# Weight differences formed in the attention part, and a third expert computed by quarter products

## The chip, the core and the metric

The kernel runs on one core of a Trainium2 chip. The core has a matrix engine (TensorE, PE in the profile), a vector engine (VectorE, DVE), a scalar engine (ScalarE, ACT), GpSimd (POOL) and a sync engine (SP); each has its own queue of instructions, and SP's queue here does nothing but issue DMAs. The metric is the device time of one launch in microseconds, as the median of several runs. A profile of one further execution shows each instruction with its times.

## The reference

```python
x = attention(q_l, k_l, v_l, q_g, k_g, v_g)     # 8 x 544 tokens, 512 columns
P = sinkhorn(exp(x @ w_gate), 8 rounds)          # 4352 tokens x 8 experts
out = 0
for e in range(8):
    h = maximum(x @ w1[e], 0)                    # 512 -> 1024
    out += P[:, e:e+1] * (h @ w2[e])             # 1024 -> 512
```

The attention has 8 batches of 8 heads with 512 local and 32 global positions; the local queries see a band of 32 positions on each side and the global ones. The routing matrix `P` multiplies every expert's output, so all eight experts work on all tokens.

## The kernel before

**First part.** A loop over 32 steps `s` (8 batches of 4 head pairs, `HP = 4`) does the attention. It is written out by hand: each step issues scores, exponentials, transposes and value products for three neighbouring head pairs on the engines, and at fixed places `f1(...)` puts in a piece of the first layer of experts 0 to 3, whose hidden rows `hT` (line 471 on ACT, 473 on DVE) are kept for later: `hd<-hT` on SP, line 475. The loads of the next batch are issued at the end of a step. The first layers' weights of experts 4 to 7 are copied into a 16-bit array in DRAM, `w1d`, by `load_w1d`, one expert in each of the batches 3 to 6. `hT` tiles, and some others, take turns in the four slots of `hpool` (tag `hT`). Then come the sinkhorn rounds, with the rest of the first layers of experts 0 to 3 between them.

**Second part.** 72 units (m, e): nine groups `m` of 512 tokens (the last has 256), and in each the experts in `ORDER = (4, 0, 5, 1, 6, 2, 7, 3)`. Even units are the experts 4 to 7, whose first layer is still to be computed; odd units are the experts 0 to 3, whose hidden rows are loaded from DRAM (`load_h`) and scaled by `P` (`scale_h`, one DVE instruction of 4.4 us, or two halves). An even unit and the odd one after it are called a pair here. While the second layer of a pair runs on PE (`product`, line 928, seven products `q` for each unit after a Strassen-like scheme), the first layer of the next even unit is put between its products. Ahead of a unit's products DVE forms its sums (`sums`: two instructions into `s`, part 0, and two in place in `h`, part 1). The results stand in seven PSUM banks over a whole group; with the last odd unit of a group (`closes`) ten DVE instructions (`add`, line 944) bring them into the output tile. The first product of the next group into a bank waits for the bank's `add`.

The first layer of an even unit can be done in two ways:

- *plain* (`l1`, line 818): 32 matmuls of 512 columns, each block evacuated by ACT;
- *by quarter products* (`Fast`, line 836): two halves `p`, each of 7 products of 4 matmuls of 256 columns. The half `p = 0` runs within the even unit of the pair before, `p = 1` within the odd one. It needs four differences of its inputs on DVE (`sums_x`: tiles `t5`, `t6`, `t4` and one in place) and seven blocks of weights and weight differences, loaded as one tile `w1q` from `w1c`. In each half `s0` forms the products H and Q, ACT copies both (`K`, line 852; `t5`, line 854), `s1` goes on in K and in H, and DVE then writes X = H + `t5` (line 861). `s2` goes on in the same bank H, which X reads, and DVE writes Y (line 868); `s3` ends H.

`fast(i)` tells which units take the second way: by `WX = {6: 2, 7: 2}` those of experts 6 and 7 from group 2 on, 12 units. The four blocks of weight differences of each of the experts 6 and 7 and each half are made in group 1: four loads of 128 KB into a slot of `w1e` (line 726), four DVE instructions (`prep_w1`, by the helper `tt`, line 689), and a store to `w1c` on GpSimd's queue (line 741).

The order of the work is that of the program text. The tile framework only adds the waits. If a unit is plain and the next even one is by quarter products, the even step's order is:

```python
if not fast(i):
    sums(i + 1, part=(0,))      # DVE
f.s0(); product(i, 3); f.s1()   # X on DVE at the end of s1
product(i, 4); product(i, 5)
f.s2()                          # PE, in the bank that X reads
```

Of the kernel before, what the change touches and what calls it, by code (L numbers as in the profile page):

```python
# [9 lines left out]
FP16 = mybir.dt.float16  # L10
FP32 = mybir.dt.float32
AF = mybir.ActivationFunctionType
ALU = mybir.AluOpType
# [10 lines left out]
def kernel(  # L24
# [13 lines left out]
    nc = tc.nc  # L38
# [3 lines left out]
    D, E = moe_w_gate.shape  # L42
    F = moe_w1.shape[2]
    P = 128
# [6 lines left out]
    HP = H // 2  # L51
# [23 lines left out]
    xd = [ydram.tile([P, DP, n], FP16, name=f"xd{m}") for m, (_, n) in enumerate(groups)]  # L75
    w1d = [ydram.tile([P, DP, F], FP16, name=f"w1d{e}") for e in range(NL, E)]
    pd = ydram.tile([E, NTOK], FP32, name="pd")
    WX = {6: 2, 7: 2}
    w1c = {e: [ydram.tile([P, 7, 2, 256], FP16, name=f"w1c{e}_{p}") for p in range(2)] for e in WX}
    psx = ExitStack()  # L80
    xpool = psx.enter_context(tc.tile_pool(name="xpool", bufs=1, side="right"))
# [10 lines left out]
    with tc.tile_pool(name="att_c", bufs=1) as att_c, \  # L92
# [308 lines left out]
        def st_G1(b, g):  # L401
            n0 = HP * b + 2 * g
            qg = qgbd[(2 * b + g) % 2]
            gc = slice(Sg * b, Sg * (b + 1))
            sg = ps_po.tile([P, 2 * 512], FP32, tag="po")
            for c0, c1, k0 in ((0, Sl - W, 2 * W), (Sl - W, Sl, W), (Sl, S, None)):
                for pr in range(2):
                    rhs = kgT[:, 2 * g + pr, gc] if k0 is None else kTe[(n0 + pr) % NK][:, k0 : k0 + c1 - c0]
                    nc.tensor.matmul(sg[:, c0:c1], qg[:, pr, :], rhs, start=(pr == 0), stop=(pr == 1))
            m2 = att_wk.tile([P, 4], FP32, tag="m2")  # L410
            nc.vector.reduce_max(out=m2[:, 0:1], in_=sg[:, 0:S], axis=AX.X)  # L411
            nc.vector.tensor_scalar(out=m2[:, 1:2], in0=m2[:, 0:1], scalar1=-scale, scalar2=None, op0=ALU.mult)
            Pg = att_wk.tile([P, S], FP16, tag="Pg")
            nc.scalar.activation(out=Pg, in_=sg[:, 0:S], func=AF.Exp, scale=scale, bias=m2[:, 1:2],
                                 accum_out=m2[:, 2:3])
            gs[(b, g)] = (Pg, m2)
# [60 lines left out]
        def load_w1e(e):  # L477
# [2 lines left out]
            wts[e] = pool.tile([P, DP, F], FP16, name="w1e", **kw)  # L480
            nc.gpsimd.dma_start(out=wts[e], in_=moe_w1[e].rearrange("(dko dki) f -> dki dko f", dki=P))

        def load_w1d(e):
            nc.gpsimd.dma_start(out=w1d[e - NL], in_=moe_w1[e].rearrange("(dko dki) f -> dki dko f", dki=P))

        fill = [(k % NL, k // NL) for k in range(NL * (B + 1))]
        n1 = 0
# [100 lines left out]
        for s in range(HP, NU + 1):  # L588
# [65 lines left out]
                logits(NJ * ((s - 5) // HP), NJ)  # L654
            if g1:
                st_G1(*gn)
            if s < NU and b + 1 < B:
                if hp == 0:
                    load_qk(b + 1, 0, (nc.sync, nc.sync))
                    load_qk(b + 1, 1, (nc.sync, nc.sync))  # L660
                elif hp == 1:
                    cast_qk(b + 1, 0, gq)
                    if b >= NL - 1:
                        load_w1d(b + 1)
                elif hp == 2:
                    vq = load_v(b + 1)
                    run(vq[:3])
                    cast_qk(b + 1, 1, gq)
                else:
                    run(vq[3:])  # L670
# [17 lines left out]
    def tt(out, in0, in1, op):  # L688
        nc.vector.tensor_tensor(out=out, in0=in0, in1=in1, op=op)  # L689
# [16 lines left out]
        return i < NUN and units[i][0] < B and units[i][0] >= WX.get(units[i][1], B)  # L706

    wseq = [(i, p) for i in range(0, NUN, 2) for p in ((0, 1) if fast(i) else (None,))]
    for j, (e, p) in enumerate((e, p) for e in WX for p in range(2)):
        wseq.insert(wseq.index((E + 2 * j + 2, None)), (e, "raw", p))  # L710
    raw = {}
    wnext = 0

    def load_w1(used):
        nonlocal wnext
        while wnext < len(wseq) and (wnext < 2 or wseq[wnext - 2] in used):
            i, *p = wseq[wnext]
            if p[0] is None:
                w = w1s[i] = wpool.tile([P, DP, F], FP16, tag="w1e", name="w1s")
                nc.sync.dma_start(out=w, in_=w1d[units[i][1] - NL])  # L720
            else:
                w = wpool.tile([P, 7, 2, 256], FP16, tag="w1e", name="w1q")
                if p[0] == "raw":
                    for o, r, k in ((0, 0, 0), (1, 0, 1), (3, 1, 0), (2, 1, 1)):
                        f0 = 512 * r + 256 * p[1]
                        nc.sync.dma_start(out=w[:, o], in_=w1d[i - NL][:, 2 * k : 2 * k + 2, f0 : f0 + 256])
                    raw[wseq[wnext]] = w
                else:
                    nc.sync.dma_start(out=w, in_=w1c[units[i][1]][p[0]])
                    w1s[(i, p[0])] = w  # L730
            wnext += 1
            if wnext < 2:
                return

    def prep_w1():
        for k in list(raw):
            w = raw.pop(k)
            for o, a, b, op in ((5, 0, 3, ALU.subtract), (3, 3, 2, ALU.add), (4, 3, 0, ALU.subtract),
                                (6, 1, 4, ALU.subtract)):
                tt(w[:, o], w[:, a], w[:, b], op)  # L740
            nc.gpsimd.dma_start(out=w1c[k[0]][k[2]], in_=w)
            used.add(k)

    def load_pb(*us):
        us = [i for i in us if i < NUN]
# [327 lines left out]
    for i, (m, e) in enumerate(units):  # L1073
        if i == NUN - 1:
            last_pair(i)
        elif i % 2 == 0:
# [44 lines left out]
            else:  # L1121
# [1 line left out]
                h = hs[i + 1]  # L1123
                s = ss[i + 1] = xsp.tile([P, HF, n], FP16, tag="xs", name="sl")
                tt(s, h[:, 0:HF, 0:n], h[:, HF:FT, 0:n], ALU.add)
            if m > 0:
                prep_w1()
            scale_x(i + 4)
            if m == 0:
                for e in {2: (2,), 4: (7,), 6: (3,)}.get(i, ()):  # L1130
# [83 lines left out]
```

## Time and profile before

| what | value |
|---|---|
| median of 3 runs | 1045.3 us (1044.04 to 1048.0) |
| profiled execution, own time | 1044.08 us |
| its span in the trace | 1042.2 us |
| PE / DVE / ACT / POOL busy in the span | 97% / 83% / 49% / 13% |
| first part, to the last first-layer matmul of experts 0 to 3 | 0 to 396 us |
| groups 1 to 7 of the second part | 491 to 1017 us |

In the profile's listings, a row of a window gives its stretch, its length and the busy microseconds of PE, of PE's weight loads, of DVE, ACT and POOL with their numbers of instructions, then the granted share of PE's clock, the busy share of the DMA engines and what they moved in GB/s. A row of the chain gives start, length and work. A row of a timeline gives start, length, engine, line, operation, tiles, and in brackets the idle time ahead of it and what ended it. `L689` is the line of the helper `tt`, so DVE's `L689` rows are told apart by their tiles.

### The profile page before, as it was taken

The numbers are of one execution on the slowest core, as the hardware profiler recorded it, in microseconds if no ns is written. First come the engines' busy times: TensorE is split into PE (matmuls) and PEld (weight loads), VectorE is DVE, ScalarE is ACT, GpSimd is POOL, SyncE is SP. The second block draws the span as 40 slices with busy tenths as digits, with TensorE's granted clock in tenths as the row PEclk, the third lists the DMA queues.
The fourth block names the chain that finished last, engine by engine and source line by source line (L and its number), as shares of the span: only waits on it lengthen the run. The fifth ranks groups of instructions, "written<-read, shape, count | busy, mean of one in ns | idle before, by whom it ended". The sixth has DMA issues, their size and how long they took to land.

```text
span 1042.2 us, 22693 instructions
## 1 busy us (share of the span) xinstructions
PE 1015.2 (97%) x9142; PEld 728.5 (70%) x9142; DVE 868.7 (83%) x1638; ACT 513.0 (49%) x1296; POOL 139.7 (13%) x227
## 2 busy tenths in 40 slices
PE   7899999999999999999999999999999999999998
PEld 4555555555555466777777877877877878878887
DVE  7687777777776786999889799889899898898895
ACT  7777878787876675223222333333333332332331
POOL 7442423414312102000000000000000000000000
PEclk9899999999999999999999999999999999999999
DMA  9887588988945999946756546454553555464470
GB/s 260 197 217 207 118 273 181 220 232 177 258 136 142 275 261 302 259 143 203 272 194 234 189 153 219 160 189 180 200 189 138 203 187 168 172 218 152 145 260 26
DMA packets 101960, 206.08 MB, mean 198 GB/s; under 512 B 33936, under 2 KB 68192, under 8 KB 90592
## 3 DMA queue, kind: packets, MB, share of 16 engines
q1 hardware_dynamic: 56064, 162.75, 45.1%
q0 software_dynamic: 43184, 32.26, 17.7%
q10 hardware_dynamic: 2608, 9.64, 2.4%
q8 instruction: 71, 1.16, 0.4%
q14 instruction: 33, 0.27, 0.1%
HBM read 168.64 MB, written 57.29 MB: 217 GB/s over the span
## 4 chain that ended last, share of the span: by engine, by line
PE 83%; ACT 8%; DVE 6%; issue 2%; DMA 1%; SPq 0%; POOL 0%; ACTq 0%; DVEq 0%
PE m L928 28%; PE ph L818 15%; PE ph L468 15%; PE pm L928 11%; PE pf L836 7%; ACT Pu L311 4%; DVE Pu L348 3%; PE ptw L359 1%; ACT hT L471 1%; ACT qbd L285 1%; PE pv L157 1%; PE pt L275 1%; DMA vraw<-in_v_l_dram 1%; PE po L380 1%; DVE m L411 1%
## 5 line engine op out<-in xcount | busy, mean ns | idle before, releaser
L468 PE MATMUL ph<-xT,w1e 128*128 128x512 f16 (+1 forms) x1152 | 255.9, 367 | 0.2
L928 PEld LDWEIGHTS <-h 128*128 128x128 f16 x2160 | 211.4, 98 | 36.6
L820 ACT ACTIVATE h<-ph 128x512 f16<-128x512 f32 (+1 forms) x192 | 107.5, 562 | 204.2 <-PE ph L818 202.2
L928 PE MATMUL m<-w2c,s 128*128 128x256 f16 x1620 | 199.9, 273 | 0.0
L928 PEld LDWEIGHTS <-s 128*128 128x128 f16 x1620 | 158.5, 98 | 30.5
L818 PE MATMUL ph<-xs,w1s 128*128 128x512 f16 (+1 forms) x768 | 174.6, 361 | 0.0
L468 PEld LDWEIGHTS <-w1e 128*128 128x128 f16 x1152 | 105.4, 98 | 96.1 <-issue 3.0
L689 DVE TENSOR_TENSOR h<-h,pb 128x2048 f16<-128x2048 f16 (+1 forms) x48 | 152.4, 3175 | 3.8 <-DMA h<-hd 3.7
L689 DVE TENSOR_TENSOR s<-h 128x1024 f16<-128x1024 f16 (+2 forms) x166 | 126.4, 803 | 24.3 <-PE m L928 16.9
L928 PE MATMUL m<-w2c,h 128*128 128x256 f16 x1080 | 137.2, 273 | 0.0
L471 ACT ACTIVATE hT<-ph 128x512 f16<-128x512 f32 (+1 forms) x192 | 104.4, 559 | 47.5 <-PE ph L468 45.2
L928 PE MATMUL pm<-w2c,h 128*128 128x256 f16 x1080 | 123.8, 273 | 0.0
L818 PEld LDWEIGHTS <-w1s 128*128 128x128 f16 x768 | 75.1, 98 | 52.6
L843 ACT ACTIVATE h<-pf 128x512 f16<-128x512 f32 x96 | 55.0, 596 | 84.1 <-PE pf L836 79.9
L311 ACT ACTIVATE Pu<-ms,mx 128x160 f16<-128x160 f32 x224 | 93.6, 420 | 5.2 <-DVE mx L308 2.7
L473 DVE TENSOR_SCALAR hT<-ph 128x512 f16<-128x512 f32 x96 | 66.1, 688 | 31.3 <-PE ph L468 30.5
L689 DVE TENSOR_TENSOR h<-h 128x1024 f16<-128x1024 f16 (+1 forms) x166 | 90.3, 586 | 0.0
L689 DVE TENSOR_TENSOR xs<-xg,pb 128x2048 f16<-128x2048 f16 (+1 forms) x36 | 78.1, 2169 | 12.8 <-DMA pb<-pd 12.8
L947 POOL DMA_DIRECT2D out_dram<-o x8 | 6.1, 758 | 533.3 <-DVE o L944 533.3
L308 DVE CUSTOM_DVE_ANT_0 ms<-sc,mask 128x160 f32<-128x160 f32 x224 | 59.9, 319 | 18.7 <-PE sc L303 18.2
L836 PEld LDWEIGHTS <-w1q 128*128 128x128 f16 x672 | 65.7, 98 | 7.7
L852 ACT COPY pf<-pf 128x512 f32<-128x512 f32 x24 | 13.7, 570 | 81.5 <-PE pf L836 81.5
(165 smaller groups left out, 1225.7 us busy)
## 6 DMA issues: line engine op xcount, KB each, us to landing
h<-hd SPq DMA_DIRECT2D x32, 1024.0 KB
hd<-hT SPq DMA_DIRECT2D x26, 1024.0 KB
w1s<-w1d SPq DMA_DIRECT2D x24, 1024.0 KB
w1q<-w1c SPq DMA_DIRECT2D x24, 896.0 KB
pb<-pd SPq DMA_DIRECT2D x64, 256.0 KB
w2c<-in_moe_w_dram POOLq DMA_DIRECT2D x16, 512.0 KB, 20.1
out_dram<-o POOLq DMA_DIRECT2D x8, 1024.0 KB, 4.6
f<-in_q_l_dram SPq DMA_DIRECT2D x15, 512.0 KB
```

The lines of the kernel that those rows point to most:

```text
L308: nc.vector.tensor_tensor_reduce(out=ms[:, ii, :], in0=sc[:, SW * ii : SW * (ii + 1)], in1=mask[:, mi, :], scale=-scale, scalar=BIG, op0=A ...
L311: nc.scalar.activation(out=d["Pu"][:, i, :], in_=ms[:, ii, :], func=AF.Exp, scale=-1.0, bias=d["mx"][:, i : i + 1], accum_out=d["sm"][:, i ...
L348: nc.vector.tensor_tensor(out=d["Pu"][:, i0:i1, 0:KW], in0=d["Pu"][:, i0:i1, 0:KW], in1=d["rs"][:, i0:i1].unsqueeze(2).to_broadcast([P, i1 ...
L468: nc.tensor.matmul(ph[:, 0:n], wts[e][:, dk, P * fm : P * (fm + 1)], xT[m][:, dk, :], start=(dk == 0), stop=(dk == DP - 1))
L471: nc.scalar.activation(out=hT[:, fm, 0:n], in_=ph[:, 0:n], func=AF.Relu)
L473: nc.vector.tensor_scalar(out=hT[:, fm, 0:n], in0=ph[:, 0:n], scalar1=0.0, scalar2=None, op0=ALU.max)
L689: nc.vector.tensor_tensor(out=out, in0=in0, in1=in1, op=op)
L818: nc.tensor.matmul(ph[:, 0:n], w1s[i][:, dk, P * fm : P * (fm + 1)], xss[i][:, dk, 0:n], start=(dk == 0), stop=(dk == DP - 1))
L820: nc.scalar.activation(out=hs[i][:, fm, 0:n], in_=ph[:, 0:n], func=AF.Relu)
L836: nc.tensor.matmul(bank[:, 256 * c : 256 * (c + 1)], self.w[:, self.sta[q], k, P * c : P * (c + 1)], self.mov[q][:, k], start=(first and c ...
L843: nc.scalar.activation(out=self.h[:, k : k + 2, 256 * c : 256 * (c + 1)], in_=bank.rearrange("p (k t) -> p k t", k=2), func=AF.Relu)
L928: nc.tensor.matmul(pm[:, HD * t : HD * (t + 1)], lhs[0][:, k, lhs[1] + P * t : lhs[1] + P * (t + 1)], w[:, k, q - 1, :], start=(k == 0 and ...
```

## The change

`WX` becomes `{6: 1, 7: 1, 5: 1}`: experts 5, 6 and 7 are computed by quarter products, each from group 1 on (21 units; `w1c` has six tiles in place of four). The differences of the weights are no longer made in group 1 (`prep_w1` and the raw entries of `wseq` go), but in the attention loop, in steps 16 to 28, for six tiles `wq` that take their turns in the slots of `hT`: in an even step the four loads on SP, at the end of the next step two DVE instructions, at the end of the one after it the other two and the store to `w1c` on SP, ahead of the next tile's loads and of the next batch's loads. `load_w1d` copies the experts in the order 6, 7, 5, 4 in place of 4, 5, 6, 7.

```diff
-    WX = {6: 2, 7: 2}
+    WX = {6: 1, 7: 1, 5: 1}
...
+        W1D = list(WX) + [e for e in range(NL, E) if e not in WX]
+
         def load_w1d(e):
             nc.gpsimd.dma_start(out=w1d[e - NL], in_=moe_w1[e].rearrange("(dko dki) f -> dki dko f", dki=P))
+
+        wqs = [(e, p) for e in WX for p in range(2)]
+        wqt = {}
+
+        def wq_load(j):
+            if 0 <= j < len(wqs):
+                e, p = wqs[j]
+                w = wqt[j] = hpool.tile([P, 7, 2, 256], FP16, tag="hT", name="wq")
+                for o, r, k in ((0, 0, 0), (1, 0, 1), (3, 1, 0), (2, 1, 1)):
+                    f0 = 512 * r + 256 * p
+                    nc.sync.dma_start(out=w[:, o], in_=w1d[e - NL][:, 2 * k : 2 * k + 2, f0 : f0 + 256])
+
+        def wq_sums(j, part):
+            if 0 <= j < len(wqs):
+                w = wqt[j]
+                for o, a, b, op in ((5, 0, 3, ALU.subtract), (3, 3, 2, ALU.add), (4, 3, 0, ALU.subtract),
+                                    (6, 1, 4, ALU.subtract))[2 * part : 2 * part + 2]:
+                    nc.vector.tensor_tensor(out=w[:, o], in0=w[:, a], in1=w[:, b], op=op)
+
+        def wq_store(j):
+            if 0 <= j < len(wqs):
+                e, p = wqs[j]
+                nc.sync.dma_start(out=w1c[e][p], in_=wqt[j])
...
             if g1:
                 st_G1(*gn)
+            j, odd = divmod(s - 4 * HP, 2)
+            if odd:
+                wq_sums(j, 0)
+            else:
+                wq_sums(j - 1, 1)
+                wq_store(j - 1)
+                wq_load(j)
             if s < NU and b + 1 < B:
...
-                        load_w1d(b + 1)
+                        load_w1d(W1D[b - NL + 1])
...
-    for j, (e, p) in enumerate((e, p) for e in WX for p in range(2)):
-        wseq.insert(wseq.index((E + 2 * j + 2, None)), (e, "raw", p))
-    raw = {}
...
-                if p[0] == "raw":
-                    for o, r, k in ((0, 0, 0), (1, 0, 1), (3, 1, 0), (2, 1, 1)):
-                        f0 = 512 * r + 256 * p[1]
-                        nc.sync.dma_start(out=w[:, o], in_=w1d[i - NL][:, 2 * k : 2 * k + 2, f0 : f0 + 256])
-                    raw[wseq[wnext]] = w
-                else:
-                    nc.sync.dma_start(out=w, in_=w1c[units[i][1]][p[0]])
-                    w1s[(i, p[0])] = w
+                nc.sync.dma_start(out=w, in_=w1c[units[i][1]][p[0]])
+                w1s[(i, p[0])] = w
...
-    def prep_w1():
-        for k in list(raw):
-            w = raw.pop(k)
-            for o, a, b, op in ((5, 0, 3, ALU.subtract), (3, 3, 2, ALU.add), (4, 3, 0, ALU.subtract),
-                                (6, 1, 4, ALU.subtract)):
-                tt(w[:, o], w[:, a], w[:, b], op)
-            nc.gpsimd.dma_start(out=w1c[k[0]][k[2]], in_=w)
-            used.add(k)
...
-            if m > 0:
-                prep_w1()
             scale_x(i + 4)
```

## The prediction

> **What bounds the kernel now.** First the page's busy times, then windows by stage. The attention stage is read over two steps (the row at 177.68), the second part by group (group 1 without quarter products; group 3 with two units of them).
>
> ```profile
> span 1042.2 us, 22693 instructions
> PE 1015.2 (97%) x9142; PEld 728.5 (70%) x9142; DVE 868.7 (83%) x1638; ACT 513.0 (49%) x1296; POOL 139.7 (13%) x227
> ...
> 177.68:198.35 20.67, 20.23 (x231) 11.51 (x229) 15.83 (x56) 16.74 (x53) 5.60 (x8) 1.00 0.94 268
> ...
> 490.66:567.20 76.54, 76.54 (x579) 56.37 (x577) 67.09 (x71) 21.50 (x36) 2.38 (x4) 1.00 0.64 233
> 642.14:717.09 74.95, 74.95 (x627) 61.06 (x625) 66.64 (x81) 25.39 (x44) 0.75 (x1) 1.00 0.53 183
> ```
>
> In the groups PE never idles. DVE works 67 to 68 us of 75, so it is second, and its load is not even. That is seen in the chain and in DVE's timeline of group 3. The chain shows the only entry from a plain to a quarter-product unit (650.00: s0, product 3, s1, products 4 and 5, then s2 at 654.37), and the turn from group 3 to 4, where group 4's first even step begins at 705.82.
>
> ```profile
> 650.00 0.87 PE pf L836 x8
> 650.88 0.87 PE m L928 x8
> 651.75 0.87 PE pf L836 x8
> 652.62 1.75 PE m L928 x16
> 654.37 0.87 PE pf L836 x8
> ...
> 697.96 3.49 PE pm L928 x32
> 701.45 4.37 PE m L928 x40
> 705.82 2.59 PE ph L818 x12
> ```
>
> ```profile
> 652.73 0.70 DVE L861 TENSOR_TENSOR pf<-pf,c 128x512 f32<-128x512 f32 x1 [0.86 <-PE pf L836]
> ...
> 693.57 2.29 DVE L689 TENSOR_TENSOR xs<-xg,pb 128x2048 f16<-128x2048 f16 x1 [0.43 <-DMA pb<-pd]
> 696.65 4.42 DVE L689 TENSOR_TENSOR h<-h,pb 128x4096 f16<-128x4096 f16 x1 [0.79 <-DMA h<-hd]
> ...
> 705.13 5.07 DVE L944 SCALAR_TENSOR_TENSOR o<-m,o 128x512 f32<-128x512 f32 x8
> 710.11 1.82 DVE L689 TENSOR_TENSOR s<-h 128x2048 f16<-128x2048 f16 x2
> ```
>
> The reader is to see two things. At the entry, X (L861) waits 0.86 us for PE and ends at 653.43, 0.94 us before s2 needs it. At the turn of the group the ten adds end only at 710.20, 4.38 us after the next even step has begun. Today that is harmless: a plain step follows, which asks nothing of DVE so early. With expert 5 in `WX`, the entry comes right there.
>
> **The change part by part.**
>
> *Quarter products for nine more units.* Groups 1 and 3 differ by two such units: (76.54 - 74.95) / 2 = 0.79 us each on PE, which is the path. Nine: **-7.1 us**.
>
> *The entry behind the closing adds,* once in each of the groups 1 to 7. Let E be the start of a group's first even step. s2 is wanted at E + 4.37 (654.37 - 650.00). DVE's order there is: adds, part 0 of `sums` (1.73 us, 710.11 to the next instruction at 711.85), X (0.70). s2 goes on in the bank that X reads, and PE takes its matmuls in order, so PE stands until X has ended. The adds end behind E by 4.28, 2.53, 3.09, 4.38, 3.81, 3.83 and 3.76 us at the seven turns (for group 3: 710.20 - 705.82). They come later still: `sums_x` for the new unit, four instructions of 1.6 us together (715.37 to 716.97 in the timeline), now stands ahead of the closing pair's `scale_h`, and only the waits for `h<-hd` absorb some of it (0, 0.79, 0.43, 0.29, 0.40 us in groups 2 to 6; 0.78 us of waits in group 0). Group 3: 4.38 + 1.6 - 0.79 + 1.73 + 0.70 - 4.37 = 3.25 us. Likewise groups 2, 4, 5, 6 and 0: 2.75, 3.04, 3.20, 3.02, 3.16; for group 1, whose pairs change, their mean of 3.05. Sum **+21.5 us**. Lower bound: the smallest lag, 2.53, with the largest absorption, at all seven: 1.5 x 7 = 10. Upper: the largest with none: 4.0 x 7 = 28. I take the sum of the rows themselves.
>
> *The first of two pairs by quarter products.* A group now has two pairs with such units on both sides, and in the first one the late half of `scale_h` (2.2 us) and three of the `sums_x` fall together. In group 3, X of expert 7's half at 671.94 had waited 1.08 us; 2.2 us more work ahead of it makes `sums` about 0.3 us late for product 5, and X then just meets s2. **+2.1 us** in seven groups; bounds 0 and 2.2 x 7 = 15. I take the sum because it is DVE's own order with its own durations.
>
> *Differences in the attention loop.* 24 DVE instructions of 0.42 us (the same ones take 6.8 us for 16 today), two at the end of each of 12 steps. Only work is added, so there is no gain; at most all of it is path: 24 x 0.45 = 10.7 us. DVE idles 4.84 us in two steps (20.67 - 15.83) and two insertions ask for 1.7. At the end of an even step DVE then waits 1.22 us for scores anyway, which covers 0.85; after an odd one it idles 0.34, so scores begin about 0.5 us late, six times. Of these 3.0 us I take half, **+1.5 us**, near the low end, because DVE has idle time later in each step.
>
> *DMAs there.* Six times four loads of 128 KB and a store of 896 KB go through SP: 8.4 MB in a stage whose DMA share is 0.80 to 0.95. The store waits for DVE and stands ahead of the next tile's loads, and at every other one ahead of the next batch's q and k loads, which get some 4 us later (257.17 today; the store waits for DVE until about 259.4, and its issue and the four loads' take 2.4 us). Their conversion on POOL starts 11 us after their issue today (257.17 and 268.23), so it starts on time or up to 2 us late, and behind it on POOL stand only `load_w1d` and, 9 us on, the next `Pl`. `wq` loads have 9 us until DVE reads them. A `wq` takes one of four `hT` slots, so a `hT` finds its slot later, but those stores are 7 us or more old, except one of 2 us. Nothing is charged; if that cover fails, DVE waits stand directly in the steps (a rival below).
>
> *The rest.* Group 1 loses 16 DVE instructions, 16 loads and four stores (0.54 us of POOL each); PE was full there (76.54 of 76.54), so nothing is won beyond room on DVE. The new order of `load_w1d` leaves expert 4 issued near 270 us and first read after 396: nothing. In the groups, 18 loads of 896 KB replace nine of 1 MB at a DMA share of 0.5 to 0.65: hidden.
>
> *The clock.* PE's stops of 3 us are new in the groups. These rows show what sparse work did near the start: two rows with PE busy 2.17 of 4 us, and the granted clock fell to 0.50.
>
> ```profile
> 10.00:12.00 2.00, 0.87 (x5) 0.39 (x5) 1.27 (x5) 2.00 (x12) 1.53 (x2) 1.00 1.12 362
> ...
> 28.00:30.00 2.00, 0.83 (x16) 0.80 (x15) 1.60 (x5) 2.00 (x13) 0.00 (x0) 1.00 1.10 231
> 30.00:32.00 2.00, 1.34 (x42) 1.14 (x41) 1.95 (x10) 1.95 (x7) 0.96 (x2) 1.00 1.12 240
> ...
> 40.00:42.00 2.00, 2.00 (x18) 0.83 (x13) 1.17 (x3) 1.88 (x6) 0.29 (x1) 0.50 1.05 196
> 42.00:44.00 2.00, 2.00 (x14) 0.97 (x13) 0.99 (x4) 0.54 (x1) 2.00 (x3) 0.79 1.10 205
> ```
>
> The clock came back after about 2.8 us of full PE (40.0 to 42.8). So a drop at an entry, with dense work behind it, costs about half of 2.8: 1.4 us. Bounds: 0 at every entry (the row of 10 to 12 us was sparse too, at 1.00) and 5.1 x 7 = 36 (half of the 10.2 us that the drop lasted). I take a drop at half of the seven: **+4.9 us**. [...]
>
> Sum: -7.1 + 21.5 + 2.1 + 1.5 + 4.9 = +22.9 us. The profiled execution took 1044.1 us, so 1067.0; the median of the runs is 1.2 us above it: **1068 us**.
>
> **Rivals.**
> - *The clock falls at every entry* (chance 0.15): 9.8 in place of 4.9, **1073 us**. For it: a stop of 3 us leaves less work around it than the rows of 28 to 32 us hold. Against: sparse rows at full clock. [...]
> - *Shorter stops* (0.16): lags as at the end of group 1, 1.5 us at each entry, and no drop of the clock: 1045.3 - 7.1 + 10 + 2.1 + 1.5 = **1052 us**. For it: loads of `h` and `pb` set part of DVE's lag and may land earlier. Against: in group 2 none was waited for, and the adds were still 3.09 us late.
> - *DVE bounds the groups as a whole* (0.09): quarter products add about 4.1 us of DVE per unit (X and Y twice at 0.70, 1.3 net of `sums_x`). If DVE keeps its idle 7 us per group, a group takes 79 us, +4.1 six times and +6.8 in group 1: +31 with the attention's 1.5, with the clock **1082 us**. Against: late DVE work loses its waits.
> - *The attention stage pays in full* (0.08): 10.7 in place of 1.5: **1077 us**. For it: PE is busy 20.23 of 20.67 us and any wait shows. Against: DVE's idle time.
> - *No stop at all, faster* (0.07): if X is on time, the change is worth -7.1 + 0.5 = **1039 us**. Decided at one point: the adds must end by E + 1.94. Against: they end at E + 2.5 or later already.
>
> **Numbers.** The forecast's chance is 0.45. A measurement of this kernel tells about 0.5% from no change, 5.2 us. The faster case gives 0.07 and 0.01 of the short stops with it; within 0.5% lies the low end of the short stops, 0.04; the rest, 0.88, is slower. The range of 1050 to 1080 us leaves out the faster case, the case of a DVE-bound whole, and 0.04 of edges.
>
> **What would show it.** In the changed kernel's chain, DVE's L944, `s` and X lines appear once per group; PE idles near 3 us ahead of s2 in each group's first even step, waiting for X; groups 1 to 7 last about 77.5 us in place of 75. The clock's rows tell whether it fell there. Attention steps keep 20.7 us per two. I am wrong if X is on time at a group's start, or if the stage between 178 and 302 us grows by more than 5 us.

## The result, and the profile after

The changed kernel takes 1086.2 us (median of 4 runs, 1081.5 to 1093.2) against 1045.4 us for the kernel before in the same comparison: a ratio of 1.040, with a 95% interval of 1.038 to 1.043. It is slower by 40.8 us by the medians and by 42 by the ratio, where 23 were forecast. The profiled execution took 1088.6 us; its span is 1086.9 us, 44.7 us longer than before's 1042.2.

Line numbers have moved: `tt` is L721 now, the quarter products L850, X L875, Y L882, `product` L942 and `add` L958. A unit whose first layer is done by quarter products is called a quarter unit below; an entry is the first even step of a group, and the turn is the passage from one group to the next.

The head of the page, and the busy times by stage (columns as in the tables before: length, then PE, PEld, DVE, ACT and POOL busy, the granted clock, DMA share, GB/s). The first row is one step of the attention stage, the second group 4, from the end of one group's closing adds to the next:

```profile
span 1086.9 us, 23423 instructions
...
PE 1027.3 (95%) x9358; PEld 755.2 (69%) x9358; DVE 908.3 (84%) x1763; ACT 531.8 (49%) x1332; POOL 139.0 (13%) x223
```

```profile
202.20:217.10 14.90, 11.42 (x107) 6.11 (x106) 9.19 (x32) 10.13 (x34) 4.30 (x9) 0.89 1.16 202
735.43:815.60 80.17, 76.62 (x648) 64.07 (x648) 71.81 (x94) 27.54 (x48) 0.75 (x1) 0.98 0.49 181
```

A group that was full of PE work before (76.54 of 76.54 and 74.95 of 74.95) now has 3.6 us without any, and its granted clock is below 1.00. The attention step took 10.3 us before (200.7 to 211.0).

The chain of waits shows what the groups lose. Its first part is the turn from group 3 to 4, its second the first pair with quarter products on both sides:

```profile
734.75 0.68 DVE o L958
735.43 1.73 DVE s L721 x2
737.16 0.62 DVE pf L875
737.78 0.04 issue
737.82 1.03 PE pf L850 x8
738.86 3.13 PE m L942 x16
741.98 0.72 PE pf L850 x4
742.71 3.49 PE pm L942 x32
...
769.15 0.94 DVE s L721 x2
...
779.01 0.62 DVE pf L882
779.63 0.04 issue
779.68 0.60 PE pf L850 x4
```

At the entry the chain runs through DVE: the last closing add, part 0 of `sums`, X (L875), and only then does s2 (L850) start. PE has stood still for 3.07 us by then. The matmuls behind it are slow as well: sixteen that take 1.75 us elsewhere take 3.13. In the pair from 761.04 to 780.27 PE waits for DVE twice, at product 5 (`s`, 775.3) and at s3 (Y, L882, 779.68). Counted from one matmul's start to the next, less the 0.109 us between starts in dense work, that is 0.3 and 0.6 us; pairs that wait for nothing last 18.33 us, this one 19.23.

The granted clock explains the slow matmuls. Two neighbouring stretches of 3.41 us, same columns:

```profile
735.61:739.02 3.41, 1.20 (x11) 1.07 (x11) 3.41 (x6) 0.13 (x1) 0.75 (x1) 1.00 0.59 245
739.02:742.44 3.42, 3.42 (x19) 2.44 (x17) 3.42 (x3) 1.07 (x2) 0.00 (x0) 0.50 0.16 62
```

The first holds most of the stop, at full clock; in the second PE works all the time, at half of it. Such a fall stands behind six of the seven entries (behind one it lasts 6.83 us, behind the others 3.41).

In the attention stage, whose last matmul (L468) ends at 405.0 instead of 395.9 us, DVE's timeline at the second odd step and SP's queue before it show a wait that before did not have (start, duration, what; in brackets the idle time ahead and what ended it):

```profile
208.43 0.15 DVE L412 TENSOR_SCALAR m<-m 128x1 f32<-128x1 f32 x1
211.17 0.89 DVE L504 TENSOR_TENSOR wq<-wq 128x512 f16<-128x512 f16 x2 [2.59 <-DMA wq<-w1d]
211.97 0.68 DVE L361 COPY pw<-ptw 128x1024 f16<-128x1024 f16 x1
```

```profile
199.29 0.32 SPq L509 DMA_DIRECT2D w1c<-wq  x1
199.67 4.70 SPq L497 DMA_DIRECT2D wq<-w1d  x4
```

The four `wq` loads stand in SP's queue behind the store of the tile before, which waits for DVE; SP issues them from 199.67 on, over 4.70 us, and DVE, which has reached the differences at 208.58, gets them at 211.17. PE then stands still from 210.18 to 213.19 (its next transposes need `Pg`, which is behind the differences on DVE), and from 213.37 to 216.79 the clock is at half.

Together, in the profiled executions:

| where | us |
|---|---|
| nine more quarter units | -7.1 |
| stops ahead of s2, seven entries (2.92, 3.07, 3.04, 3.07, 3.07, 3.07, 2.80) | +21.0 |
| clock at half behind six of them (11.1 us less between 404 us and the end in the run that has no fall there, below) | +11.1 |
| first pair of quarter products on both sides, 7 x 0.9 | +6.3 |
| attention stage, with its own fall of the clock (about 1.7) | +9.1 |
| one late load of quarter weights (group 6) | +1.35 |
| sum | +41.8 |
| measured by the spans | +44.7 |

The 3 us left over are mostly a matter of counting. From one matmul's start to the next, as above, the seven stops are 22.2 us and not 21.0, and the late load is 1.5. Nine shorter waits in the groups, of 0.16 to 0.43 us, two of them for quarter weights and the others near the closing adds, come to 2.0 us.

### The profile page after: what moved, and what is told of

Same layout as the page of the kernel before. It is cut to its first block, busy times and chain, and to the rows that moved or that the text cites. A ratio compares the mean times of both kernels' runs of the same rounds, so it can differ in the third digit from the quotient of the medians.

```text
span 1086.9 us, 23423 instructions
## 1 busy us (share of the span) xinstructions
PE 1027.3 (95%) x9358; PEld 755.2 (69%) x9358; DVE 908.3 (84%) x1763; ACT 531.8 (49%) x1332; POOL 139.0 (13%) x223
## 4 chain that ended last, share of the span: by engine, by line
PE 54%; DVE 28%; DMA 7%; ACT 5%; issue 4%; SPq 1%; DVEq 0%; ACTq 0%
PE m L942 15%; PE ph L468 13%; PE pf L850 9%; DVE h L721 7%; PE pm L942 7%; DVE s L721 4%; DVE o L958 3%; PE ph L832 3%; DVE Pu L348 3%; DMA w1q<-w1c 3%; ACT Pu L311 2%; DMA pb<-pd 2%; DMA wq<-w1d 2%; DVE xs L721 2%; PE pt L275 1%
## 5 line engine op out<-in xcount | busy, mean ns | idle before, releaser
L468 PE MATMUL ph<-xT,w1e 128*128 128x512 f16 (+1 forms) x1152 | 257.2, 368 | 0.2
L942 PEld LDWEIGHTS <-h 128*128 128x128 f16 x2160 | 211.4, 98 | 31.6 <-issue 0.5
L942 PE MATMUL m<-w2c,s 128*128 128x256 f16 x1620 | 208.5, 279 | 0.4
L857 ACT ACTIVATE h<-pf 128x512 f16<-128x512 f32 x168 | 97.2, 596 | 183.1 <-PE pf L850 151.3
L942 PEld LDWEIGHTS <-s 128*128 128x128 f16 x1620 | 161.5, 100 | 30.4 <-DVE s L721 2.3
L468 PEld LDWEIGHTS <-w1e 128*128 128x128 f16 x1152 | 105.6, 98 | 97.1 <-issue 4.6
L721 DVE TENSOR_TENSOR h<-h,pb 128x2048 f16<-128x2048 f16 (+1 forms) x57 | 153.1, 2695 | 1.8 <-DMA h<-hd 1.8
L850 PEld LDWEIGHTS <-w1q 128*128 128x128 f16 x1176 | 116.2, 99 | 45.4 <-issue 27.3
L942 PE MATMUL m<-w2c,h 128*128 128x256 f16 x1080 | 138.6, 273 | 0.0
L721 DVE TENSOR_TENSOR s<-h 128x1024 f16<-128x1024 f16 (+2 forms) x184 | 128.2, 738 | 7.2 <-ACT h L834 5.9
L942 PE MATMUL pm<-w2c,h 128*128 128x256 f16 x1080 | 123.8, 273 | 0.0
L850 PE MATMUL pf<-xs,w1q 128*128 128x256 f16 x672 | 96.4, 278 | 22.9 <-DVE pf L875 21.0
L834 ACT ACTIVATE h<-ph 128x512 f16<-128x512 f32 (+1 forms) x120 | 64.5, 541 | 108.0 <-PE ph L832 105.9
L832 PE MATMUL ph<-xs,w1s 128*128 128x512 f16 (+1 forms) x480 | 103.7, 351 | 0.0
L311 ACT ACTIVATE Pu<-ms,mx 128x160 f16<-128x160 f32 x224 | 93.6, 420 | 12.2 <-DVE mx L308 10.3
L721 DVE TENSOR_TENSOR h<-h 128x512 f16<-128x512 f16 (+1 forms) x184 | 92.1, 542 | 0.0
L721 DVE TENSOR_TENSOR xs<-xg,pb 128x2048 f16<-128x2048 f16 (+1 forms) x36 | 78.0, 2166 | 13.8 <-DMA hd<-hT 8.1
L850 PE MATMUL pf<-t,w1q 128*128 128x256 f16 x504 | 76.7, 275 | 3.0 <-DVE pf L882 3.0
```

The costliest lines, as they stand in the source:

```text
L311: nc.scalar.activation(out=d["Pu"][:, i, :], in_=ms[:, ii, :], func=AF.Exp, scale=-1.0, bias=d["mx"][:, i : i + 1], accum_out=d["sm"][:, i ...
L468: nc.tensor.matmul(ph[:, 0:n], wts[e][:, dk, P * fm : P * (fm + 1)], xT[m][:, dk, :], start=(dk == 0), stop=(dk == DP - 1))
L832: nc.tensor.matmul(ph[:, 0:n], w1s[i][:, dk, P * fm : P * (fm + 1)], xss[i][:, dk, 0:n], start=(dk == 0), stop=(dk == DP - 1))
L834: nc.scalar.activation(out=hs[i][:, fm, 0:n], in_=ph[:, 0:n], func=AF.Relu)
L850: nc.tensor.matmul(bank[:, 256 * c : 256 * (c + 1)], self.w[:, self.sta[q], k, P * c : P * (c + 1)], self.mov[q][:, k], start=(first and c ...
L857: nc.scalar.activation(out=self.h[:, k : k + 2, 256 * c : 256 * (c + 1)], in_=bank.rearrange("p (k t) -> p k t", k=2), func=AF.Relu)
```

## The experiments

Each was compared with the kernel before, which ran on the same chip beside it; 1.040 is the changed kernel's ratio.

**X ahead of part 0 of `sums`**

```diff
-                if not fast(i):
-                    sums(i + 1, part=(0,))
...
                     f.s1()
+                    sums(i + 1, part=(0,))
                     product(i, 4)
```

> In the entry step part 0 of sums (1.73 us of DVE) is queued behind X instead of ahead of it; all else is as in the changed kernel (1086.2 us). My theory: PE's stop ahead of s2 is DVE's lag, so it shrinks from about 3.0 to about 1.3 us at each of the seven entries, -12 us; and the fall of the granted clock (3.4 us at half speed behind six of seven stops, about 1.8 us lost each) hangs on the length of the stop, so it goes too, another -11 us: about 1063 us, with no row below full clock between 493 and 1050 us. Rival A: the clock falls at these places whatever the length of the stop (the entry's small matmuls, or any stop): -12 alone, 1074 us. Rival B: something other than DVE's order sets X (a bank, ScalarE's copy of Q): no change, 1086 us.

Measured: 1071.5 us, ratio 1.026 (1.024 to 1.028). The stop ahead of s2 fell to 1.34 us (0.62 and 1.06 in groups 1 and 7), and between 216 and 1060 us the clock never fell (mean granted clock of the execution 0.995, against 0.981 in the changed kernel's). But a second stop of 0.76 us came at each entry. The chain there:

```profile
803.79 0.61 DVE pf L875
804.40 1.20 DVE s L721 x2
...
806.04 1.29 DVE h L721 x2
807.33 0.62 DVE pf L882
807.95 0.04 issue
807.99 0.60 PE pf L850 x4
```

X comes right behind the adds, but part 0 now stands ahead of Y (L882), for which s3 waits. By its time alone this run lies nearer to rival A's 1074 us than to the theory's 1063, but the clock's rows decide against A. So DVE's order sets both stops, the fall of the clock goes with the long stop, and what I had not counted is that work taken from ahead of one wait lands ahead of the next: 14.9 us back (the ratios' difference times 1044) instead of 23.

**Matmuls that fill a part of the stop**

```diff
+        def fill(self):
+            t = self.tile("r2")
+            for k in range(8):
+                nc.tensor.matmul(t, self.w[:, 0, k % 2, 0:P], xss[self.i][:, k % 4, :], start=True, stop=True)
...
+                    f.fill()
                 f.s2()
```

> The changed kernel (1086.2 us) with eight matmuls of 128x512 more (1.75 us) ahead of s2 in each entry step, whose product nobody reads: X comes as late as before, but PE idles only about 1.3 of the 3.05 us. My theory, that the fall of the clock is caused by PE's idling: no fall, and 6 x 1.8 us less, about 1075 us, with groups of 78.4 instead of 80.3 us. Rival A, that the clock falls for another reason (the rise of load behind the stop, time since the last fall): 1086 us. Rival B, that the eight matmuls end behind X and hold s2 up: above 1086 us.

Measured: 1075.5 us, ratio 1.030 (1.028 to 1.032). PE idles 1.07 to 1.35 us ahead of s2, X is as late as it was, and no row between 404 us and the last matmul is below full clock (mean granted clock of the execution 0.998). Group 3:

```profile
649.41:728.44 79.03, 76.34 (x656) 63.91 (x655) 71.74 (x95) 27.54 (x48) 0.75 (x1) 1.00 0.52 184
```

Eight matmuls whose product nobody reads made the kernel 11 us faster by the ratios. That is the price of the clock alone, apart from the stop's: by the spans, from the end of the attention stage on, 681.8 us became 670.8. The rival that the clock falls for another reason is out.

**Both parts of the `wq` sums at the end of the even step**

```diff
-            if odd:
-                wq_sums(j, 0)
-            else:
+            if not odd:
+                wq_sums(j - 1, 0)
                 wq_sums(j - 1, 1)
                 wq_store(j - 1)
```

> The changed kernel (1086.2 us), but in the attention stage all four differences of a wq tile are made at the end of the even step, two steps after its loads were issued and just ahead of its store, instead of two of them already at the end of the odd step. My theory: most of that stage's 9.1 us (last matmul of the stage at 405.0 instead of 395.9 us) comes from DVE waiting in its queue for the loads at the odd step (4.2 us in three waits) and from what hangs on it (Pg's scaling and PE behind it), so the stage gives back 5 to 7 us: 1079 to 1081 us. Rival A: the DMAs and their queue order are the cost (q and k loads and casts behind the store): under 2 us back, 1084 us or more. Rival B: DVE's added 10 us of work is the cost wherever it stands: no change.

Measured: 1078.9 us, ratio 1.033 (1.032 to 1.035), 7.3 us back. The stage's last matmul ends at 397.5 us instead of 405.0, 1.5 later than before. The same DVE work and the same DMAs are there, so neither of them costs that much by itself, as the two rivals had it: it was the place of the first two differences, at the end of an odd step, where they come sooner behind their loads and ahead of other work. The window that answers to the row of 14.90 us above:

```profile
200.40:211.50 11.10, 9.68 (x107) 5.54 (x106) 9.63 (x38) 9.73 (x34) 4.31 (x9) 1.00 1.26 268
```

**The loads ahead of the store**

```diff
             else:
+                wq_load(j)
                 wq_sums(j - 1, 1)
                 wq_store(j - 1)
-                wq_load(j)
```

> The changed kernel (1086.2 us) with one order changed in the attention stage: at the end of an even step, SP issues the four loads of the next wq tile first, and DVE's second two differences and the store of the tile before follow. The first two differences stay in the odd step. The loads then no longer stand behind a store that waits for DVE. My theory: in the odd steps' cost (1.4, 4.7, 0.4, 0.9, 0.2 and 1.5 us at the six ends, together 9.1) the waits for loads (2.6, 0.6 and 1.0 us in DVE's queue) and the fall of the clock behind the first of them (1.7 us) go, and what stays is DVE's 0.85 to 2 us of work in front of the next scores: the stage's last matmul comes at about 400 us instead of 405.0, and the kernel takes about 1081 us. Rival: the loads are slow themselves (512-byte pieces in a stage whose DMA queues are nearly full), whatever stands ahead of them: 1085 us or more.

Measured: 1081.2 us, ratio 1.034 (1.031 to 1.036). The last matmul of the stage comes at 398.5 us, and the step that took 14.9 takes 10.6. SP's queue:

```profile
196.34 3.13 SPq L497 DMA_DIRECT2D wq<-w1d  x4
199.57 0.42 SPq L509 DMA_DIRECT2D w1c<-wq  x1
```

In the odd steps DVE waits for the loads no more. The stage began 1.6 us earlier in this execution (178.5 against 180.1), so 4.9 of its 6.5 us are the edit's, and SP begins to issue these loads 1.7 us earlier within the stage. By the same count the run before leaves 1.9 us. So, by these two runs, of the 9.1 us about 5 were the wait for loads that stood behind a store, with the fall of the clock behind it, 2.3 the place of DVE's differences in front of the next scores, and 1.9 stay in either place. Why SP took 4.70 us to issue four loads there, and 3.13 here, is open.

**The attention part alone**

```diff
     def fast(i):
-        return i < NUN and units[i][0] < B and units[i][0] >= WX.get(units[i][1], B)
+        return i < NUN and units[i][0] < B and units[i][0] >= {6: 2, 7: 2}.get(units[i][1], B)
```

> Only the attention part of the change: the six wq tiles are loaded, summed and stored there, but the groups use quarter products for the same units as the kernel before (experts 6 and 7 from group 2; expert 5's differences are stored and not used). My theory: the parts add up, so this is the kernel before (1045.4 us) plus the attention stage's 9.1 us, about 1054.5 us, with groups as long as before and no fall of the clock in them. Rival: part of the 9.1 us is not the attention part's own (chance of that execution, whose clock fell once in that stage): 1047 to 1052 us.

Measured: 1053.8 us, ratio 1.009 (1.008 to 1.011), 9.9 us slower. The attention stage ends at 405.6; the groups last as long as before (74.8, 75.5, 76.0, 74.7 us; before 74.8, 75.5, 76.2, 74.4), and the clock does not fall in them (1.00 from 643.54 to 719.50). The parts add up, and the 9.1 us was no accident of one execution.

**Without the late half of `scale_h`**

```diff
-                if late:
-                    scale_h(i + 2, HF, FT)
                 sums_x(i + 3, (7, 6))
```

> The changed kernel (1086.2 us) without the late half of scale_h in the first of a group's two pairs that are quarter products on both sides and in the pair after it (2.29 us of DVE each). This leaves out part of the computation: the upper half of those hidden rows is not scaled by the routing weight. My theory: the 0.9 us that the first such pair loses (0.47 at product 5, whose sums come late, and 0.43 at s3, which waits for Y) is this instruction's place in DVE's queue, so the pairs become 18.3 us long (product 6 of the odd step to that of the next one, 19.23 now) and the seven groups give back 7 x 0.9 = 6 us: about 1080 us; the stop of 3.05 us and the falls of the clock stay, since DVE has 3.6 us of idle time ahead of the entry's quarter products anyway, unless the 2.29 us let the closing adds come earlier too. Rival: DVE's queue as a whole is late (71.8 us of work in a group of 80.2), so that every microsecond taken off DVE shortens the groups: 2 x 2.29 x 7 = 32 us less, about 1054 us.

Measured: 1061.6 us, ratio 1.016 (1.015 to 1.018), between the two expectations. The first pair lost nothing any more, as my theory had it; but the stops fell too, to 1.65 us in six of seven groups, and with them the clock's falls. Group 3:

```profile
647.24:723.20 75.96, 74.31 (x650) 63.40 (x649) 67.60 (x92) 27.45 (x48) 0.75 (x1) 1.00 0.54 191
```

So the stop depends on how much DVE has to do before the turn, not on the ten adds and part 0 alone. From a group's last Relu of a quarter unit (in this run the one that starts at 776.44) to X, DVE's chain has no wait of more than half a microsecond: scaling, sums, adds, X. Whatever is taken off that stretch comes off the stop.

**Quarter products for experts 6 and 7 alone, from group 1 on**

```diff
-    WX = {6: 1, 7: 1, 5: 1}
+    WX = {6: 1, 7: 1}
```
(and the `wq` sums together, as above)

> Quarter products for experts 6 and 7 alone, from group 1 on (two units more than the kernel before, not nine), with the wq sums together at the end of the even step. No entry then stands behind a group's closing adds, and no group has two pairs of quarter products on both sides. My theory, that the loss of the change lies in these two and in the early sums: 1043.9 to 1045.4 (the kernel before) - 2 x 0.79 + about 1.0 for four tiles in the attention stage: 0.5 us faster than the kernel before, within what can be told. Rival: quarter products in group 1 or the weights' loads bring a loss of their own: 1048 us or more.

Measured: 1044.4 us, ratio 0.9999 (0.999 to 1.001). Without expert 5 no entry stands behind the closing adds, and the whole loss is gone; four tiles cost 1.7 us in the attention stage (397.6 against 395.9), about what two quarter units win.

**Another order at the entry, all three experts**

```diff
                     f.s1()
+                    if m > 0:
+                        add(i - 1, 1, old)
+                        store(m - 1)
                     product(i, 4)
                     product(i, 5)
-                    sums(i + 1, part=(1,))
                 f.s2()
+                if not fast(i):
+                    sums(i + 1)
...
+                if closes(i) and q == 1 and fast(i + 3):
+                    old = fixed[q]
-                if q >= 6 or closes(i):
+                elif q >= 6 or closes(i):
                     add(i, q, fixed[q])
```
(part 0 is no longer in its old place, the group's store follows the deferred adds, and the `wq` sums are together)

> The changed kernel with the wq sums together at the end of the even step (attention stage about 7.3 us shorter, as measured) and another order on DVE at a group's entry: the closing pair's last two adds (product 1, 1.25 us) and both parts of sums stand behind X, as X, two adds, Y, sums. My theory: the stop of 3.05 us is DVE's queue ahead of X, so it falls by 1.73 + 1.25 to about 0.1 us, and no fall of the clock is left: 1086.2 - 7.3 - 21 - 11 = about 1047 us; of the units' gain of 7.1 us the first pair of quarter products on both sides takes back 6.3 and the attention stage 1.5, so that the kernel stands level with the one before (1045). Rival: once PE does not stop at the entry, DVE (71.8 us of work in a group that would take 75) is late everywhere behind it, and 10 us or more come back as other waits: 1057 us or more.

Measured: 1052.1 us, ratio 1.007 (1.006 to 1.009), between the theory (1047) and the rival (1057). No stop over 0.3 us is left at the entry, the clock stays at 1.00, and a group takes 75.9 us:

```profile
638.37:714.23 75.86, 75.23 (x651) 63.16 (x649) 71.69 (x95) 27.54 (x49) 0.75 (x1) 1.00 0.53 191
```

DVE is busy 71.7 of these 75.9 us. In the first pair PE still idles 0.43 us for Y in each group, and in three groups PE waits 0.45 to 0.89 us for quarter weights, whose load takes 10.2 us from the moment its buffer is free. So the order of the work, at the entry and in the attention stage, gives back all but 7.7 us.

**Work moved to POOL**

```diff
                 if late:
-                    scale_h(i + 2, HF, FT)
+                    scale_h(i + 2, HF, FT, nc.gpsimd)
```
```diff
-                tt(t[q], a, b, ALU.subtract)
+                nc.gpsimd.tensor_tensor(out=t[q], in0=a, in1=b, op=ALU.subtract)
```

The late half, the differences of `sums_x`, and both, each in the kernel of the run before:

> The kernel with sums together and another order at the entry (1052.1 us), whose late half of scale_h (2.29 us of DVE, two in each of the groups 1 to 7) is done by POOL, which is idle in the groups (0.75 us of 80). Without those two instructions on DVE the groups of the changed kernel took 75.96 instead of 80.2 us. If POOL works beside DVE: the pairs lose their 0.9 us no longer, 1052.1 - 6.3 = about 1046, and down to 1042 if the closing adds come earlier too. Rival: POOL takes longer than the 5.6 us from its issue to the first use of that half (its product of 128x256 took 0.76 us in the attention stage, so 128x2048 may take 6), or slows DVE beside it (0.42 to 1.02 us for one difference beside POOL's casts): 1055 us or more.

> The same kernel (1052.1 us) with sums_x, twelve differences of 128x512 in a group (0.42 to 0.48 us each on DVE, 5.3 us together), on POOL. If POOL works beside DVE, DVE loses 5.3 of 71.8 us and the waits behind it go: 1044 to 1047 us. Rival: POOL is two to three times slower at each and slows DVE while it works, so that the differences are late for the products that take them: 1055 us or more.

> Both of them on POOL: about 9.9 us of DVE less in a group. If the two work side by side: PE is full in the groups, 1045.4 - 7.1 + 1.5 = about 1040 us, 0.5% below the kernel before. [...]

Measured: 1109.4, 1090.4 and 1126.9 us (ratios 1.063, 1.044 and 1.081, with intervals of 1.060 to 1.065, 1.042 to 1.047 and 1.075 to 1.086). All three are slower than the kernel of 1052.1 us that they start from; the rivals named for the first two were right, by more than they had asked. POOL's and DVE's timelines where POOL had the late half:

```profile
758.07 4.48 POOL L823 TENSOR_TENSOR h<-h,pb 128x2048 f16<-128x2048 f16 x1 [18.13 <-DVE s L720]
```

```profile
759.12 4.57 DVE L720 TENSOR_TENSOR h<-h 128x1024 f16<-128x1024 f16 x2
763.62 2.28 DVE L720 TENSOR_TENSOR xs<-xg,pb 128x2048 f16<-128x2048 f16 x1
```

POOL takes 4.48 us where DVE takes 2.28, and the two DVE differences beside it, 1.28 us elsewhere (at 760.17 in the changed kernel), take 4.57. They end at 763.69, and POOL ends at 762.55: 1.14 of their 1.28 us come after it, so by these rows they hardly moved until POOL was done. PE stood still for 3.51 us at one place (700.08 to 703.59).

**The routing weights in 16 bits**

```diff
-    pd = ydram.tile([E, NTOK], FP32, name="pd")
+    pd = ydram.tile([E, NTOK], FP16, name="pd")
...
-        t = xsp.tile([P, 512], FP32, tag="pb", name="pb") if us else None
+        t = xsp.tile([P, 512], FP16, tag="pb", name="pb") if us else None
...
-        pts = xsp.tile([3 * NT, 3, P], FP32, tag="xs", name="pts")
+        pts = xsp.tile([3 * NT, 3, P], FP16, tag="xs", name="pts")
```

In the changed kernel, in the one with another order at the entry, and in the kernel before:

> The changed kernel (1086.2 us), whose routing weights pd and pb are kept in 16 bits instead of 32, and nothing else. In the changed kernel's profile a DVE product of 128x2048 with the 32-bit pb takes 2.28 us and a sum of 128x2048 of 16-bit operands alone 1.22 us, so a group's DVE work should fall by about a fifth (71.8 to 58 to 60 us), with the order as it stands. My theory, DVE's load: the closing adds are then no longer 4.3 us behind the next group's first step, the stop falls below 1 us, the clock does not fall in the groups, the first pair loses nothing: 1045.4 - 7.1 + 9.1 (attention stage as it is) = about 1047 us, at most 1053. Rival A, the order alone (ten adds, then part 0, then X, counted from the last product): the stop stays at 1.5 us or more in each group: 1058 us or more. Rival B: products with broadcast operands are not faster in 16 bits: 1086 us.

> The kernel with sums together and another order at the entry (1052.1 us), with pd and pb in 16 bits. If DVE's load is what was left: PE is full in the groups, so 1045.4 - 7.1 + about 2 for the attention stage = 1040 us, faster than the kernel before by about 0.5%. Rival: the loads of the quarter weights (10.2 us from the slot's release to the landing, with PE waiting 0.5 to 0.9 us for them in half of the groups) keep 3 to 5 us: 1044 us.

> The kernel before (1045.4 us) with pd and pb in 16 bits. PE is full in its groups, so DVE's relief is worth nothing there: 1044 to 1046 us, no difference that can be told. Rival: the stretch ahead of the groups and the last pair, where DVE's products are on the path, give 2 us or more: 1043 us or less.

Measured: 1055.6 us (ratio 1.011, 1.009 to 1.013), 1040.3 us (0.9963, 0.9951 to 0.9975) and 1044.1 us (1.0001, 0.9992 to 1.0011). The two products with `pb`, from the list of DVE's groups by shape, in the first of them (line, engine, operation, names and shapes, count; busy, mean ns):

```profile
L721 DVE TENSOR_TENSOR h<-h,pb 128x2048 f16<-128x2048 f16 x46 | 55.4, 1216 | 1.9 <-DMA h<-hd 1.9
...
L721 DVE TENSOR_TENSOR xs<-xg,pb 128x2048 f16<-128x2048 f16 x32 | 38.9, 1217 | 12.2 <-ACT hT L471 7.6 <-DMA pb<-pd 4.6
```

These took 2283 and 2285 ns in the changed kernel, where `pb` was the only operand of 32 bits; a sum of 128x2048 in 16 bits takes 1217 ns in both. So the one 32-bit operand had cost these products nearly half of their speed.

One group of each of the three, the changed kernel first, then the one with another order, then the kernel before (a group with two quarter units, the others have three):

```profile
643.15:718.01 74.86, 74.31 (x650) 63.39 (x649) 59.38 (x94) 27.46 (x49) 0.75 (x1) 1.00 0.48 180
```
```profile
631.45:705.60 74.15, 74.15 (x650) 63.39 (x649) 59.60 (x93) 27.35 (x49) 0.75 (x1) 1.00 0.49 182
```
```profile
633.80:708.75 74.95, 74.95 (x626) 61.06 (x625) 55.49 (x82) 25.39 (x44) 0.77 (x1) 1.00 0.46 169
```

In the changed order 0.55 us of stop per group remain (2.31 in group 1, 0.55 in six): that much is the order, the other 2.5 was DVE's load. With both mended PE never idles in the group, which takes 0.80 us less than one with a quarter unit fewer: the price of 0.79 us per unit holds. The first of the three was to be at most 1053 us and took 1055.6. The attention stage was counted there, with 9.1 us (it cost 9.5); not counted were the 5.6 us of stops and the loads of quarter weights that PE waited 0.88 and 0.83 us for in two groups. The second is faster than the kernel before by 0.37% (0.25 to 0.49), and the third shows that this is not the 16-bit weights by themselves: 1040.3 against 1044.1 us.

## Why the prediction was wrong

The direction and the largest term were right; the time lay above the range.

- *The entry behind the closing adds, +21.5:* right, 21.0 (22.2 from start to start). The lag worked out from DVE's order gave 2.75 to 3.25 us for the six entries I could work out, and the trace has 2.80 to 3.07. Row by row it is off by up to 0.3 us either way, so that the sum is this near is in part luck. The instructions behind it were the ones named, L958, `s` and X. What the sum did not say is that the lag is DVE's load over the 24 us before X (777.05 to 800.80 in the run without the late half); the runs without the late half and with 16-bit weights showed that.
- *Nine more quarter units, -7.1:* right, 0.80 us per unit where nothing else stands in the way.
- *The first of two pairs by quarter products, +2.1:* the mechanism was right (`sums` late for product 5, Y late for s3), the size was not: 0.9 us in place of 0.3, 6.3 in all. I had let X "just meet" s2 and had not followed DVE's order two instructions further, to Y.
- *Differences in the attention loop, +1.5:* wrong, 9.1. Two steps failed. "`wq` loads have 9 us until DVE reads them" was right as a cover (199.67 to 208.58), but no time to landing was set beside it: in the step that lost most, what the first difference reads was there at 211.05, 11.4 us after SP began to issue the four loads. SP took 4.70 us to issue them, where four of the same kind took 1.9 to 2.1 in group 1 of the kernel before, and it began late because they stand behind a store that waits for DVE. And "DVE has idle time later in each step" did not help, since scores come first behind the differences: in place of half of 3.0 us, the six odd steps lost 1.4, 4.7, 0.3, 1.0, 0.2 and 1.5. So my own sign of being wrong came: the stage between 178 and 302 us grew by 9.0 us, more than 5. With the differences in the even steps, where I had counted 1.22 us of DVE's wait as cover, the stage cost 1.5 us (1.9 counted from its start); that this is the forecast's figure is chance, since it was worked out for another place.
- *The clock, +4.9:* a drop at half of the entries at 1.4 us. It fell at six of seven and cost 11.1 us there, 1.8 each, and once more in the attention stage. My 2.8 us of recovery came from one row near the start; here a fall lasts 3.41 us or twice that.
- *DMAs in the groups, nothing:* nearly right; 1.35 us in one group and under 0.3 in two more, and in the runs that shortened the groups, up to 1.2 us in one to three groups of each.
- *The rivals:* "the clock falls at every entry" (1073) and "the attention stage pays in full" (1077) both came true in size, nearly in full. Their grounds did not: the clock fell at six of seven entries but cost more each time, and the attention stage paid for late loads and a fall of the clock more than for DVE's own work. I had priced them as ways in which the forecast could fail one at a time; they do not exclude each other, and together with the pairs' 4.2 us they give 1068 + 6.2 + 7.6 + 4.2 = 1086. That this meets the median exactly is chance: the profiled execution, from which the sizes come, took 2.4 us more than the median. That no case held two of them is why the range ended at 1080. "DVE bounds the groups as a whole" was not the case of the changed kernel in the form I gave it (it idles 8.4 of a group's 80.2 us), but DVE's load was behind two of the terms, and once the stops were gone DVE idled 4.2 of 75.9 us. Two sums were off without effect: that rival's terms come to 32.9 us with the attention's 1.5, not 31, so about 1083 us, and 24 x 0.45 is 10.8.

## What to carry to other kernels

Where a second engine is busy 90% of a stage (here DVE, 71.8 of 80.2 us), work out its order instruction by instruction to the end of the step, not to the first wait: what is moved from ahead of one wait stands ahead of the next. A load queued behind a store that waits for an engine inherits that wait (here the four `wq` loads, issued from 199.67 us on behind the store at 199.29, and from 196.34 on once they stood ahead of it); count from there, and set the load's time to landing beside the cover that it has. Before moving work to another engine, look for an operand whose width costs the busy one time (here 2283 ns with a 32-bit `pb`, 1216 with a 16-bit one); and add up the rivals that can hold at the same time.

## What the runs showed of the hardware

*Where the clock fell.* All changes of the granted clock in the changed kernel's profile lie on a grid of 3.413 us, within 0.004 us. I divided the profile by this grid and took PE's idle share in each window. Beyond the first 45 us, all seven windows that idled 0.60 to 0.88 were followed by half clock; one of 0.30, inside the fall of 6.83 us, was followed by half too. The other windows that idled 0.36 or more, five of 0.36 to 0.43, were followed by full clock. The length of a stop alone does not tell it. Some of them (idle share of the fullest window):

```
stop (us)        length  share  next window
210.18-213.19    3.00    0.88   half
492.82-495.74    2.92    0.72   half
573.12-576.19    3.07    0.60   half
734.75-737.82    3.07    0.65   half
945.06-946.41    1.35    0.40   full
976.63-979.43    2.80    0.43   full
```

A stop of 2.80 us that two windows share left the clock alone; one of 2.92 us, most of it inside one window, halved it. The grid does not start with the program: counted back to the start of the span, it begins at 1.75 us in this profile and at 1.88 in that of the kernel before. The spread of the changed kernel's runs goes with the clock: the two with a mean granted clock of 0.991 took 1081.5 and 1083.8 us, the two with 0.981 and 0.980 took 1088.6 and 1093.2. The rows of one window and the next, in the run with the sums together:

```profile
805.65:809.07 3.42, 2.62 (x13) 1.83 (x13) 3.42 (x6) 0.72 (x2) 0.00 (x0) 0.50 0.75 307
802.24:805.65 3.41, 1.13 (x11) 0.87 (x9) 3.41 (x6) 0.00 (x0) 0.75 (x1) 1.00 0.00 0
```

The last had 2.28 us idle, and the one above it is the window behind it. In the first 45 us of the changed kernel's profile, with other and smaller matmuls, windows of 0.42 (5.16 to 8.57) and 0.57 (29.05 to 32.47) were followed by half and one of 0.43 (22.22 to 25.64) by full, so the share of idle time does not tell it alone there.

*POOL beside DVE.* Beside a POOL product of 4.48 us, in the run with the late half on POOL, two DVE differences took 4.57 us that take 1.28 in the changed kernel; and the changed kernel's first two `wq` differences (186.58 us), beside POOL's casts (186.12 to 188.34), took 0.86 and 1.14 us, where the median of the 24 is 0.425.
